# Attention scores of a decode kernel: quarters of the keys on four column groups against halves on two

## The chip, the cores and the metric

The kernel runs on one core of a Trainium2 chip. The metric is device time in microseconds (us) of that core for one launch. A core has a tensor engine (PE; its weight loads are listed apart as PEld), a vector engine (DVE), a scalar engine (ACT), GpSimd (POOL) and a sync engine (SP), which here issues all transfers; 16 DMA engines move the data. SBUF is the on-chip memory with 128 partitions; PSUM is the memory that PE writes to, in banks of 512 float32 per partition.

## The reference

One token passes four blocks, two attention layers (A) and two mixers (B), with the same weights and caches in both rounds:

```python
# A: x is (1, 1, 640); 32 heads of 192; the last W = 4096 keys of the cache
q = (x @ wq).reshape(B, Sq, Hq, Dh).transpose(0, 2, 1, 3)
scores = jnp.einsum("bhqd,bhkd->bhqk", q, k) * (Dh ** -0.5)
p = softmax(scores, axis=-1)
o = jnp.einsum("bhqk,bhkd->bhqd", p, v)
a = o.transpose(0, 2, 1, 3).reshape(B, Sq, Hq * Dh) @ wo
# B: layernorm, w1 and gelu, shifts, w2; layernorm, w3, gelu, w4
x = x + A(layernorm(x)); x = x + B(layernorm(x))
x = x + A(layernorm(x)); x = x + B(layernorm(x))
```

All tensors are bf16. With one token the shifted parts of B are zero, so the kernel computes of B only the second half (w3, gelu, w4). K and V of one head are 4096 x 192 bf16, 1536 KB each.

## The kernel before

**Storage.** Big loads go to a ring of 12 cells in SBUF, each 128 partitions x 6144 bf16 (1536 KB, one head's K or V). `take` gets a cell from the front of a queue of free cells, `give` puts it back. A load is issued by SP in the fixed order of `stream`, up to eight in flight; it waits until the last reader of its cell is done. In layer 0 the transposed K of heads 0 to 7 (`NKEEP`) is kept in eight cells, and layer 1 uses it instead of loading these heads again.

**Groups.** Heads go in eight groups of four (`QH`). Layer 0 takes the groups from the last to the first, so the kept heads are transposed in its last two groups; layer 1 from the first to the last. `attention` runs, for each group, the softmax of this group (scores done during the group before), then for each of its heads the product with V (`pv`) and, in between, the transposes and scores of the next group's heads.

**K to scores.** A cell of K has 32 keys in each partition. `transpose_quart` turns a quarter of it with one DVE instruction (L450): 128 x 768 words of 32 bit, in 32 x 32 blocks, so that a word with two neighbouring elements of a key stays whole. The result goes to a kept cell or to a quarter of the `area` cell. `scores` multiplies: the stationary operand is a 16-column block of `Qblk` (4 heads x 4 blocks of 32 keys; the other heads' columns hold zeros, so a group accumulates into one block), the moving operand are 256 elements of a turned quarter. There are `NCOL` = 6 matmuls for each quarter, and quarter q writes the 16 rows at partition 32 q of the score tile `ST_ps`. So the four quarters of a head lie in four groups of 32 partitions. T(h, half) and S(h, half) in `attention` work on two quarters at a time, and S alternates between the two. For kept heads in layer 1 one S does all four.

The tile `ST_both` (L540) is one PSUM bank, 128 partitions x 512 float32. Its left 256 columns serve one group of heads, its right 256 the next, in turn (`next_scores`).

**Softmax** (`softmax_steps`), in seven steps: `part_max`, the maximum of each row (L557, DVE); `turn_max`, a PE transpose of the 128 maxima to one row (L562); `full_max`, the maximum per head, written out again for 128 rows (L567, L572); `spread_max`, a matmul that turns it back (L580), a copy (L583), and exp with the row sums (L586, ACT); `turn_p`, a DVE transpose of P in 32 x 32 blocks, 128 x 256 bf16 (L591), and the row sums by head (L593); `swap`, 16 matmuls with 32-column parts of the identity (L605) that gather P by key into `PT`, a copy (L608), and the sums over partitions (L613); `recip`, their reciprocal.

**Values.** `pv` makes 16 matmuls of 384 columns, in four column groups (L654); DVE turns the result (L661, 128 x 384) and `o_fold` sums it (L668 or L672 and L673) into `oT`. `out_proj` and `out_row` multiply by wo.

**Order of the work.** [...] At the start of a group it is, on DVE: T(h0, 0), `part_max`, T(h0, 1), `full_max`, `turn_p`, T(h1, 0), T(h1, 1); on PE: S(h0, 0), `turn_max`, S(h0, 1), `spread_max`, a q projection and an output projection, `swap`, then `pv` of the first head, S(h1, 0), S(h1, 1), `o_fold`, `pv` of the second, S(h2, 0), and so on. Layer 1 starts with the scores of the kept heads, four of the first and four of the second group, in a row.

Of the kernel before, what the change touches and what calls it, by code (L numbers as in the profile page):

```python
# [10 lines left out]
F32 = mybir.dt.float32  # L11
U32 = mybir.dt.uint32
ACTF = mybir.ActivationFunctionType
ALU = mybir.AluOpType
AX = mybir.AxisListType
# [3 lines left out]
P = 128  # L19
# [13 lines left out]
NJ4, NGK, NM = 4, 8, 4  # L33
# [26 lines left out]
def kernel(  # L60
# [14 lines left out]
    nc = tc.nc  # L75
# [12 lines left out]
    QH = 4  # L88
    NG = H // QH
    QC = QH * Dh  # L90
    QT = QC // P
    NT = 4
    QUART = NFB * (NGK // NT) * P * 2
    FREE = NT * QUART
    scale = float(Dh) ** -0.5
    eps = 1e-5
    s0 = Sk - W
# [332 lines left out]
    area = [None, 0]  # L430
    SW = P * NGK // NT

    def transpose_quart(layer, h, q):

        if layer == 1 and h < NKEEP:
            return kept[h][:, q * QUART:(q + 1) * QUART]
        Kn = need("k", layer, h)
        NY = NFB * (NGK // NT)
        Ku = Kn[:].bitcast(U32).rearrange("p (j y b) -> p j y b", j=NJ4, b=32)
        if layer == 0 and h < NKEEP:  # L440
            if q == 0:
                kept[h] = take(("T", h))
            T = kept[h][:, q * QUART:(q + 1) * QUART]
        else:
            if area[0] is None:
                area[0] = take(("area", layer))
            T = area[0][:, area[1] * QUART:(area[1] + 1) * QUART]
            area[1] = (area[1] + 1) % NT
        Tu = T.bitcast(U32).rearrange("p (y j b) -> p j y b", y=NY, j=NJ4)
        nc.vector.transpose(Tu, Ku[:, :, q * NY:(q + 1) * NY])  # L450
        if q == NT - 1:
            give(("k", layer, h))
        return T

    def qproj_steps(c, xc, part=None, row=None):
# [29 lines left out]
        def spread():  # L485
            if row is not None:
                qT_ps = psm.tile([P, n], F32, tag="psm")
                for tl in range(n):
                    i, j = divmod(tl, n // 2)
                    nc.tensor.matmul(qT_ps[:, tl:tl + 1], lhsT=row[:, j * P:(j + 1) * P],  # L490
                                     rhs=Eq[0:33, i, 0:1], start=True, stop=True)
                held["q"] = qT_ps
            Xq = o_bytes[:, 2 * (SW + 2 * QH):][:, 0:4 * n].rearrange("p (t b) -> p t b", b=4)
            nc.vector.tensor_tensor(  # L494
                out=Xq[:], in0=held["q"][:, :].unsqueeze(2).broadcast_to([P, n, 4]),
                in1=maskq[:, :].unsqueeze(1).broadcast_to([P, n, 4]), op=ALU.mult)
            held["x"] = Xq
# [23 lines left out]

        return project, spread, repeat, block

    def scores(h, Ts, q0, ST_ps, hq):

        ng = NGK // NT
        Q = [Qblk[:, h // QH % 2, QAT[hq] + n * QSTEP:][:, 0:QW] for n in range(NCOL)]
        views = [T.rearrange("p (g f i t) -> p g f i t", f=NFB, g=ng, i=P) for T in Ts]
        for f in range(NFB):
            for t in range(2):  # L530
                n = 2 * f + t
                for i, T4 in enumerate(views):
                    r = 32 * (q0 + i)
                    nc.tensor.matmul(  # L534
                        ST_ps[r:r + QW, :].rearrange("p (g i) -> p g i", g=ng), lhsT=Q[n],
                        rhs=T4[:, :, f, :, t],
                        start=(hq == 0 and n == 0), stop=(hq == QH - 1 and n == NCOL - 1))


    ST_both = psS.tile([P, 2 * SW], F32, name="ST_ps")  # L540
    nc.vector.memset(ST_both[:], 0.0)
    turn = [0]

    def next_scores():
        turn[0] += 1
        i = turn[0] % 2
        return ST_both[:, i * SW:(i + 1) * SW]

    def softmax_steps(n, ST_ps, sc, space, bank=None):
        held = {}
        halves = space.bitcast(BF16)

        def part_max():
            pm = short("pm")
            nc.vector.tensor_reduce(out=pm[:], in_=ST_ps, op=ALU.max, axis=AX.X)  # L557
            held["pm"] = pm

        def turn_max():  # L560
            pmT_ps = psm.tile([1, P], F32, tag="psm")
            nc.tensor.transpose(pmT_ps[0:1, :], held["pm"][:, 0:1], ident[:, :])  # L562
            held["pmT"] = pmT_ps

        def full_max():
            ngm = space[0:1, SW:SW + 2 * QH]
            nc.vector.tensor_reduce(out=ngm[:], in_=held["pmT"][0:1, :].rearrange("o (q x m) -> o x q m", q=4, m=NM),  # L567
                                    op=ALU.max, axis=AX.XY, negate=True)
            held["PrT"] = halves[:, SW:2 * SW]

            wide = held["PrT"][0:1, :].bitcast(F32)
            nc.vector.tensor_scalar(  # L572
                out=wide.rearrange("o (q x m) -> o q x m", q=4, m=NM),
                in0=ngm[:].unsqueeze(1).unsqueeze(3).broadcast_to([1, 4, 2 * QH, NM]),
                scalar1=sc[0:1, 0:1], scalar2=None, op0=ALU.mult)
            held["w"] = wide

        def spread_max():
            nb_ps = psm.tile([P, 1], F32, tag="psm")
            nc.tensor.matmul(nb_ps[:], lhsT=held["w"],  # L580
                             rhs=one[0:1, :], start=True, stop=True)
            nb_sb = space[:, 289:290]
            nc.scalar.copy(nb_sb[:], nb_ps[:])  # L583
            Pr = halves[:, 0:SW]
            lpart = space[:, 288:289]
            nc.scalar.activation(out=Pr, in_=ST_ps, func=ACTF.Exp,  # L586
                                 bias=nb_sb[:, 0:1], scale=sc[:, 0:1], accum_out=lpart[:, 0:1])
            held["Pr"], held["l"] = Pr, lpart

        def turn_p():  # L590
            nc.vector.transpose(held["PrT"], held["Pr"])  # L591
            lh = space[:, 280:284]
            nc.vector.tensor_scalar(out=lh[:], in0=hm[:], scalar1=held["l"][:, 0:1], scalar2=None, op0=ALU.mult)  # L593
            held["lh"] = lh

        def swap():
            ng = NGK // NT
            if bank is None:
                PT_ps = psm.tile([P, n, NJ4, NGK], F32, tag="psm")
            else:  # L600
                PT_ps = bank[:, 0:n * NJ4 * NGK].rearrange("p (h j g) -> p h j g", j=NJ4, g=NGK)
            src = held["PrT"].rearrange("p (g j i) -> p i j g", g=ng, j=NJ4)
            for m in range(NM):
                for q in range(NT):
                    nc.tensor.matmul(PT_ps[32 * m:32 * (m + 1), :, :, ng * q:ng * (q + 1)], lhsT=Eq[:, q, :],  # L605
                                     rhs=src[:, m:QW:NM], start=True, stop=True)
            PT = big.tile([P, n, NJ4 * NGK], BF16, name="PT")
            nc.scalar.copy(PT[:].rearrange("p h c -> p (h c)"), PT_ps[:].rearrange("p h j g -> p (h j g)"))  # L608
            if bank is None:
                l_ps = psm.tile([P, QH], F32, tag="psm")  # L610
            else:
                l_ps = bank[:, 512:512 + QH]
            nc.tensor.matmul(l_ps[:], lhsT=ones, rhs=held["lh"][:], start=True, stop=True)  # L613
            held["lps"] = l_ps
            return PT

        def recip():
            lq = space[:, 284:288]
            rl = short("rl", 1, 2)
            nc.vector.scalar_tensor_tensor(out=lq[:], in0=held["lps"][:], scalar=1.0, in1=blkm[:],  # L620
                                           op0=ALU.mult, op1=ALU.mult, accum_out=rl[:, 0:1])
            nc.vector.reciprocal(rl[:], rl[:])
            return rl

        return part_max, turn_max, full_max, spread_max, turn_p, swap, recip
# [100 lines left out]
    def attention(layer, x_cur, rs_cur, x_new, z_new, rs_new, ss_new):  # L726
# [11 lines left out]
            nc.vector.tensor_scalar(out=sc[:], in0=rstd[:], scalar1=scale, scalar2=None, op0=ALU.mult)  # L738

        def T(h, half):  # L740
            for q in (2 * half, 2 * half + 1):
                if (h, q) not in Th:
                    Th[h, q] = transpose_quart(layer, h, q)

        def S(h, half, ST_ps, hq):
            if layer == 1 and h < NKEEP:
                if half == 1:
                    scores(h, [Th.pop((h, q)) for q in range(NT)], 0, ST_ps, hq)
                    give(("T", h))
                return  # L750
            scores(h, [Th.pop((h, q)) for q in (2 * half, 2 * half + 1)], 2 * half, ST_ps, hq)
            if half == 1 and layer == 0 and h == last_plain:
                give(("area", layer))
                area[0] = None
# [37 lines left out]
        for hq, h in enumerate(groups[0]):  # L792
            for half in range(2):
                if layer == 0:
                    T(h, half)
                else:
                    Th.update({(h, q): transpose_quart(layer, h, q) for q in (2 * half, 2 * half + 1)})
                S(h, half, ST, hq)
                if (hq, half) == (0, layer):
                    qb[2]()  # L800
# [317 lines left out]
```

## Time and profile before

| what | value |
|---|---|
| median of three runs | 511.95 us (511.36 to 512.05) |
| the profiled execution, its time | 511.54 us |
| its span, first to last instruction | 509.7 us |
| granted PE clock, mean | 0.723 |
| read from HBM | 214.01 MB, 420 GB/s over the span |
| score matmuls, L534 | 1536, busy 157.8 us |
| K transposes, L450 | 224, busy 201.6 us |
| PV matmuls, L654 | busy 90.2 us (largest group) |

The page divides the span into 40 slices of 12.7 us and gives for each the busy share of an engine and the rate of the transfers. A busy PE is not PE at its peak: its instructions overlap, and their ends are modelled. "Granted clock" is the share of the full PE clock. In a line of a group the fields are: source line, engine, operation, output and inputs, shape, count; then busy time and mean length in ns; then the idle time of the engine just before them and what ended it. In the lists of waits and in the chain, "DMA x" is a transfer of x that somebody waits for; in the list of transfers the last number is the median time in us from issue to landing.

### The profile page before, as it was taken

The numbers are of one execution on the slowest core, as the hardware profiler recorded it, in microseconds if no ns is written. First come the engines' busy times: TensorE is split into PE (matmuls) and PEld (weight loads), VectorE is DVE, ScalarE is ACT, GpSimd is POOL, SyncE is SP. The second block draws the span as 40 slices with busy tenths as digits, with TensorE's granted clock in tenths as the row PEclk, the third lists the DMA queues.
The fourth block names the chain that finished last, engine by engine and source line by source line (L and its number), as shares of the span: only waits on it lengthen the run. The fifth ranks groups of instructions, "written<-read, shape, count | busy, mean of one in ns | idle before, by whom it ended". The sixth has DMA issues, their size and how long they took to land.

```text
span 509.7 us, 9498 instructions
## 1 busy us (share of the span) xinstructions
PE 313.2 (61%) x4084; PEld 186.2 (37%) x4084; DVE 292.6 (57%) x604; ACT 48.9 (10%) x173; POOL 3.7 (1%) x16
## 2 busy tenths in 40 slices
PE   1056667666565555857655766767655765557685
PEld 0023333343332322534333643544322433324354
DVE  2067557666674755566723244968666656656522
ACT  1000101010010100001010101010100101001101
POOL 2000000000000000000000000000000000000000
PEclk9999756777597766576765586789887766857655
DMA  8999999999999999999999999999999999999996
GB/s 370 432 432 429 430 441 432 429 429 422 417 426 441 432 425 446 432 402 458 429 391 413 381 438 424 439 429 429 426 429 433 429 430 432 418 437 429 418 409 250
DMA packets 12014, 214.63 MB, mean 421 GB/s; under 512 B 2564, under 2 KB 3076, under 8 KB 7428
## 3 DMA queue, kind: packets, MB, share of 16 engines
q1 hardware_dynamic: 11972, 214.02, 98.5%
q8 instruction: 32, 0.52, 0.4%
q14 instruction: 10, 0.08, 0.0%
HBM read 214.01 MB, written 0.00 MB: 420 GB/s over the span
## 4 chain that ended last, share of the span: by engine, by line
DMA 60%; PE 20%; DVE 14%; issue 4%; ACT 1%; SPq 1%; DVEq 0%; ACTq 0%
DMA cell<-in_A_k_cache_dram 37%; DMA cell<-in_A_v_cache_dram 19%; DVE cell L450 9%; PE ST_ps L534 9%; PE O_ps L654 5%; DMA cell<-in_B_w_dram 4%; DVE o_sb L661 2%; PE qT_ps L480 1%; PE y_ps L1062 1%; PE nb_ps L580 1%; DVE words L557 1%; PE l_ps L613 1%; DVE V_ps L643 1%; DVE o_sb L591 1%; SPq L55 0%
## 5 line engine op out<-in xcount | busy, mean ns | idle before, releaser
L534 PE MATMUL ST_ps<-cell,Qblk 128*16 128x256 bf16 x1536 | 157.8, 364 | 110.8 <-DVE cell L450 66.6
L450 DVE STREAM_TRANSPOSE cell<-cell 128x768 uint32<-128x768 uint32 x224 | 201.6, 946 | 33.7 <-DMA cell<-in_A_k_cache_dram 31.6
L534 PEld LDWEIGHTS <-Qblk 128*16 128x16 bf16 x1536 | 84.7, 108 | 175.1 <-issue 150.2
L654 PE MATMUL O_ps<-cell,PT 128*2 128x384 bf16 x1000 | 90.2, 436 | 11.0 <-DMA cell<-in_A_v_cache_dram 9.1
L661 DVE STREAM_TRANSPOSE o_sb<-O_ps 128x384 f32<-128x384 f32 x64 | 36.7, 573 | 79.6 <-PE O_ps L654 79.5
L654 PEld LDWEIGHTS <-PT 128*2 128x2 bf16 x1024 | 41.2, 96 | 26.9 <-issue 18.7
L669 ACT ACTIVATE words<-oT_ps,words 32x6 bf16<-32x6 f32 x40 | 10.3, 257 | 163.6 <-PE oT_ps L668 150.3
L591 DVE STREAM_TRANSPOSE o_sb<-o_sb 128x256 bf16<-128x256 bf16 x15 | 6.7, 445 | 31.9 <-ACT o_sb L586 14.2
L668 PE MATMUL oT_ps<-o_sb,Lq 128*32 128x6 f32 x160 | 13.4, 192 | 10.7 <-DVE o_sb L661 10.1
L668 PEld LDWEIGHTS oT_ps<-o_sb,Lq 128*32 128x32 f32 x160 | 11.6, 137 | 20.4 <-issue 14.4
L674 ACT ACTIVATE words<-oT_ps,words 32x6 bf16<-32x6 f32 x24 | 6.2, 257 | 107.6 <-PE ST_ps L534 79.6
L480 PE MATMUL qT_ps<-words,wq_sb 128*128 128x1 bf16 x210 | 7.2, 165 | 12.9 <-DMA wq_sb<-in_A_wq_dram 12.0
L494 DVE TENSOR_TENSOR o_sb<-qT_ps,words 128x24 bf16<-128x24 f32 (+1 forms) x18 | 2.9, 163 | 20.2 <-PE qT_ps L480 17.4
L583 ACT COPY o_sb<-nb_ps 128x1 f32<-128x1 f32 x15 | 2.4, 159 | 102.2 <-PE nb_ps L580 102.2
L480 PEld LDWEIGHTS <-wq_sb 128*128 128x128 bf16 x210 | 6.8, 104 | 14.1 <-DMA wq_sb<-in_A_wq_dram 13.1
L605 PEld LDWEIGHTS <-ident 128*32 128x32 bf16 x256 | 5.8, 111 | 14.8 <-issue 14.5
L469 PE MATMUL qr_ps<-wq_sb,words 128*1 128x384 bf16 x90 | 10.7, 376 | 0.0
L700 PE MATMUL yr_ps<-cell,words 128*1 128x320 bf16 x108 | 10.4, 335 | 0.0
L673 PE MATMUL oT_ps<-o_sb,Lq 128*32 128x6 f32 x48 | 5.9, 194 | 6.8 <-DVE o_sb L672 6.8
L580 PEld LDWEIGHTS nb_ps<-words,o_sb 1*128 1x128 f32 x30 | 7.0, 287 | 7.2 <-issue 5.4
L673 PEld LDWEIGHTS oT_ps<-o_sb,Lq 128*32 128x32 f32 x48 | 5.0, 134 | 11.2 <-issue 9.1
L580 PE MATMUL nb_ps<-words,o_sb 1*128 1x1 f32 x30 | 8.2, 339 | 1.5 <-DVE o_sb L572 1.5
(159 smaller groups left out, 200.3 us busy)
## 6 DMA issues: line engine op xcount, KB each, us to landing
cell<-in_A_k_cache_dram SPq DMA_DIRECT2D x56, 1536.0 KB, 27.7
cell<-in_A_v_cache_dram SPq DMA_DIRECT2D x56, 1536.0 KB, 27.7
cell<-in_A_wo_dram SPq DMA_DIRECT2D x13, 960.0 KB, 27.5
wq_sb<-in_A_wq_dram SPq DMA_DIRECT2D x5, 1536.0 KB, 13.4
cell<-in_A_v_cache_dram SPq DMA_DIRECT2D x6, 768.0 KB, 23.7
cell<-in_B_w_dram SPq DMA_DIRECT2D x1, 1536.0 KB, 11.8
cell<-in_B_w_dram SPq DMA_DIRECT2D x2, 768.0 KB, 10.3
cell<-in_A_wo_dram SPq DMA_DIRECT2D x3, 480.0 KB, 17.0
```

Of the source, the lines that this page charges most:

```text
L450: nc.vector.transpose(Tu, Ku[:, :, q * NY:(q + 1) * NY])
L469: nc.tensor.matmul(qr_ps[32 * i:32 * i + 1, :], lhsT=xc[:, kc:kc + 1], rhs=wq_sb[:, kc, t0 * P + i * N:t0 * P + (i + 1) * N], start=(kc == ...
L480: nc.tensor.matmul(qT_ps[:, tl:tl + 1], lhsT=wq_sb[:, kc, t * P:(t + 1) * P], rhs=xc[:, kc:kc + 1], start=(kc == 0), stop=(kc == ND - 1))
L534: nc.tensor.matmul(ST_ps[r:r + QW, :].rearrange("p (g i) -> p g i", g=ng), lhsT=Q[n], rhs=T4[:, :, f, :, t], start=(hq == 0 and n == 0), s ...
L580: nc.tensor.matmul(nb_ps[:], lhsT=held["w"], rhs=one[0:1, :], start=True, stop=True)
L591: nc.vector.transpose(held["PrT"], held["Pr"])
L654: nc.tensor.matmul(O_ps[r:r + 2, :], lhsT=PT[:, hq, 2 * i:2 * i + 2], rhs=v_pair(V, h, 2 * i * Dh, 2 * Dh), start=(i < 4), stop=(i >= NB - 4))
L661: nc.vector.transpose(o_sb[:], O_ps.rearrange("p (e a c) -> p e c a", e=2, c=NA))
L668: nc.tensor.matmul(oT_ps[r, :], lhsT=Lq[:], rhs=o_sb[:, e, :, e], start=(e == 0), stop=(e == 1))
L669: nc.scalar.activation(oT[r, :], oT_ps[r, :], ACTF.Copy, scale=rl[r, 0:1])
L673: nc.tensor.matmul(oT_ps[r, :], lhsT=Lq[:], rhs=o2, start=True, stop=True)
L700: nc.tensor.matmul(yr_ps[32 * i:32 * i + 1, :], lhsT=oT[:, k:k + 1], rhs=wo_t[:, k * D + i * N:k * D + (i + 1) * N], start=(k == 0), stop= ...
```

## The change

K is turned and multiplied in halves instead of quarters, and the two groups in flight share the score bank by partitions instead of by columns:

- `NT` is 2 instead of 4. One DVE transpose turns half a head, 128 x 1536 words; a head has two of them instead of four.
- A score matmul has 512 moving columns instead of 256, and a head has 12 of them instead of 24. The half at index q0 writes 16 rows at partition ST[0] + 32 q0. So a head uses two groups of 32 partitions: 0 and 32 for one group of heads, 64 and 96 for the next.
- `ST_both` is still one bank; a group of heads has 64 partitions x 512 columns of it. `part_max`, exp and `turn_p` run on 64 partitions with 512 elements each. `turn_p` writes P turned to the other 64 partitions.
- `turn_max` turns 64 maxima, `full_max` and the spread write 64, and the sums over partitions run over 64. The short buffers of the softmax move within `o_sb`.
- `PT` comes from 8 matmuls with 64 moving columns and 64 rows, instead of 16 with 32 columns and 128 rows.

What is loaded, in which order, and the order of the steps in `attention` stay. In the core of the diff "..." marks what is left out:

```diff
-    NT = 4
-    QUART = NFB * (NGK // NT) * P * 2
-    FREE = NT * QUART
+    NT = 2
+    HP = P // 2
+    HALF = NFB * (NGK // NT) * P * 2
+    FREE = NT * HALF
...
-    def scores(h, Ts, q0, ST_ps, hq):
+    def scores(h, Ts, q0, ST, hq):
...
-                    r = 32 * (q0 + i)
+                    r = ST[0] + 32 * (q0 + i)
                     nc.tensor.matmul(
-                        ST_ps[r:r + QW, :].rearrange("p (g i) -> p g i", g=ng), lhsT=Q[n],
+                        ST_both[r:r + QW, :].rearrange("p (g i) -> p g i", g=ng), lhsT=Q[n],
                         rhs=T4[:, :, f, :, t],
...
-    ST_both = psS.tile([P, 2 * SW], F32, name="ST_ps")
+    ST_both = psS.tile([P, SW], F32, name="ST_ps")
...
-        i = turn[0] % 2
-        return ST_both[:, i * SW:(i + 1) * SW]
+        i = turn[0] % 2 * HP
+        return i, ST_both[i:i + HP, :]
...
+        at, ST_ps = ST
+        S, T = slice(at, at + HP), slice(HP - at, P - at)
...
-            nc.vector.tensor_reduce(out=pm[:], in_=ST_ps, op=ALU.max, axis=AX.X)
+            nc.vector.tensor_reduce(out=pm[S, :], in_=ST_ps, op=ALU.max, axis=AX.X)
...
-            nc.tensor.transpose(pmT_ps[0:1, :], held["pm"][:, 0:1], ident[:, :])
+            nc.tensor.transpose(pmT_ps[0:1, :], held["pm"][S, 0:1], ident[S, S])
...
+            held["PrT"] = halves[T, 0:SW]
             nc.vector.transpose(held["PrT"], held["Pr"])
...
-                    nc.tensor.matmul(PT_ps[32 * m:32 * (m + 1), :, :, ng * q:ng * (q + 1)], lhsT=Eq[:, q, :],
+                    nc.tensor.matmul(PT_ps[32 * m:32 * (m + 1), :, :, ng * q:ng * (q + 1)], lhsT=Eq[T, (HP - at) // 32 + q, :],
                                      rhs=src[:, m:QW:NM], start=True, stop=True)
...
         def T(h, half):
-            for q in (2 * half, 2 * half + 1):
-                if (h, q) not in Th:
-                    Th[h, q] = transpose_quart(layer, h, q)
+            if (h, half) not in Th:
+                Th[h, half] = transpose_half(layer, h, half)
```

## The prediction

> **What bounds the kernel now.** I read the page's first three parts, then the groups by shape, the transfers by window, the chain, and the timeline of the tensor engine (PE).
>
> ```profile
> PE 313.2 (61%) x4084; PEld 186.2 (37%) x4084; DVE 292.6 (57%) x604; ACT 48.9 (10%) x173; POOL 3.7 (1%) x16
> GB/s 370 432 432 429 430 441 432 429 429 422 417 426 441 432 425 446 432 402 458 429 391 413 381 438 424 439 429 429 426 429 433 429 430 432 418 437 429 418 409 250
> q1 hardware_dynamic: 11972, 214.02, 98.5%
> ```
>
> No compute engine is busy two thirds of the time; the transfers hold all 16 DMA engines from start to end. 214.6 MB at the usual 430 GB/s is 499 us of the 509.7 us span. So work on PE or DVE costs nothing until it releases a buffer so late that the transfer queue runs dry. What must be read is how much queue stands ahead of each release. Landing times tell it (issue to landing; windows 100 to 150 us, 249 to 250, 289 to 290 and 321 to 321.5, in this order):
>
> ```profile
> cell<-in_A_k_cache_dram SPq DMA_DIRECT2D x6, 1536.0 KB, 27.7
> cell<-in_A_v_cache_dram SPq DMA_DIRECT2D x1, 1536.0 KB, 10.9
> cell<-in_A_k_cache_dram SPq DMA_DIRECT2D x1, 1536.0 KB, 8.8
> cell<-in_A_k_cache_dram SPq DMA_DIRECT2D x1, 1536.0 KB, 13.3
> ```
>
> In steady state these transfers are issued every 3.63 us, so a landing of 27.7 means seven others in front. At 289.5 a landing takes 8.8 us, and there alone the engines visibly slack (343 GB/s in 291.9 to 295.3, below). I take 8.8 as the landing of an almost dry queue, and landing minus 8.8 as cover: 18.9 us in mid-kernel, 2.1 at 249.3, none at 289.5, 4.5 at 321.1. The cover is thin because layer 0 ends with eight cells holding kept transposed heads, so few are left to load into.
>
> Two stretches are chains of compute that wait for no data: 199.8 to 244.7 (layer 0, last groups) and 286 to 321 (start of layer 1). What the change adds there, less the cover, is lost.
>
> **The change, part by part.** Its core is the score matmuls.
>
> ```profile
> L534 PE MATMUL ST_ps<-cell,Qblk 128*16 128x256 bf16 x1536 | 157.8, 364 | 110.8 <-DVE cell L450 66.6 <-DVE words L557 38.1 <-DVE o_sb L672 4.7
> 202.01 1.45 PE L534 MATMUL ST_ps<-cell,Qblk 128*16 128x256 bf16 x12 [4.45 <-DVE words L557]
> 63.54 0.37 PE L534 MATMUL ST_ps<-cell,Qblk 128*16 128x256 bf16 x1 [1.54 <-DVE cell L450]
> 58.83 1.68 PE L534 MATMUL ST_ps<-cell,Qblk 128*16 128x256 bf16 x22
> 294.55 2.33 PE L534 MATMUL ST_ps<-cell,Qblk 128*16 128x256 bf16 x74 [0.30 <-DVE Qblk L518]
> ```
>
> (Start, length, instructions in one run.) A half of a head is 12 matmuls into two column groups (partitions r and r+32). They take 1.45 us, one alone 0.37, so (1.45-0.37)/5 = 0.216 us a pair: two groups run side by side, each a 256-column matmul per 0.216. That is at granted clock 0.50. The run of 74 has four groups at clock 1.00: (2.33-0.28)/17.5 = 0.117 us for four. So the price is columns per column group. After the change a half is 6 matmuls of 512 columns into one group: the same columns, but no partner. 6 x 0.43 = 2.6 us instead of 6 x 0.216 = 1.3 at clock 0.5: **+1.3 us a half cold, +0.65 warm**. Half as many instructions buy nothing back, since PE streams columns.
>
> Where the halves of a head are both ready, they overlap: from 58.83 on, 22 of 24 matmuls take 1.68 us, and the last two end at 60.71, 1.9 us in all, where pairs in sequence would need 12 x 0.216 + 0.2 = 2.8. I take it that the two new column groups overlap so too. [...]
>
> Prices of one step each, cold / warm:
> - (b) A later head of a group: DVE transposes both halves, PE follows. Four transposes take 3.51 us (62.55, L450); two of twice the size: 946 ns plus 768 elements at (946-727)/256 ns (768 elements at L450, 512 at L643) is 1.6 each, 3.3 in all, -0.2. Only the second half's scores are exposed: +1.3-0.2 = +1.1 / +0.45.
> - (c) The second head, whose transposes are done early: 1.9 us become 2.6+0.4 (the same stagger): +1.1 / +0.55.
> - (d) The first head: the maximum (L557) now reads 512 elements on 64 partitions instead of 256 on 128; 392 ns become some 660 by the same slope or 1 ns an element, +0.25 (0 to +0.3). In the built program the first score matmul still waits for it, though it reads the other half of the bank, so the 0.4 us of that wait are not saved. The second half stands behind the transpose of the maxima, which stands behind the first half, so both count: +2.6+0.25-0.1 = +2.7 cold; warm, 0.6 us of it fills the wait for the second transpose: +0.95. Behind it on PE queue the spread of the maximum, the next q projection and the first PV.
> - (e) The rest of the softmax: exp (L586, 564 ns for 256) at 0.8 ns an element (ACT: 468 ns for 384 at L474, 265 for 128 at L608) +0.2; the turn of P (L591, 445 ns) +0.25. PT: 8 matmuls of 64 columns for 16 of 32, equal columns, taken as 0 (-0.2, if instructions count; +0.2, if 64-row operands stall PE). +0.45.
> - (f) The eight kept heads at the start of layer 1: 24 matmuls in four groups become 12 of 512 in two: 0.7 to 1.4 us warm, 1.3 to 2.6 cold. One and a half heads run before PE warms up at 291.9: 1.5 x 1.3 + 6.5 x 0.7 = 6.5; part may fill the 0.8 us that PE idles at 296.9; I take 6.
>
> The clock decides between the ends. Windows (length, PE, PEld, DVE, ACT, POOL busy, granted clock, DMA share, GB/s):
>
> ```profile
> 66.60:70.10 3.50, 2.23 (x27) 1.21 (x23) 1.23 (x2) 0.26 (x1) 0.00 (x0) 0.50 0.99 425
> 80.30:83.70 3.40, 3.40 (x25) 1.95 (x26) 1.05 (x5) 0.81 (x3) 0.00 (x0) 0.50 1.04 448
> 83.70:87.10 3.40, 1.97 (x37) 1.09 (x33) 3.35 (x7) 0.99 (x3) 0.00 (x0) 1.00 1.07 463
> 291.90:295.30 3.40, 3.10 (x103) 2.33 (x99) 0.66 (x4) 0.12 (x1) 0.00 (x0) 0.99 0.91 343
> 199.80:244.70 44.90, 31.90 (x387) 20.29 (x387) 28.25 (x53) 3.44 (x13) 0.00 (x0) 0.62 1.00 428
> ```
>
> A stretch of 3.4 us with PE busy throughout is followed by clock 1.00; one with 65% stays at 0.50. Longer score runs fill more such stretches, so the change warms its own clock. [...]
>
> Sum, **first stretch**: it holds two of each of (b) to (e). Cold 2 x (1.1+1.1+2.7+0.45) = 10.7, warm 4.9. Now a quarter of it is warm (mean 0.62). With half warm: 7.8, less what warmth gains on today's work: a cold head step is 6.84 us (62.55 to 69.38, DVE to DVE), by 0.117 instead of 0.216 some 1.2 less; a quarter more warmth over seven such steps is -2. Less the 0.5 us that DVE waits for K at 245.7: about 5. Cover 2.1: **2.9 us lost** (ends: 0 and 8).
> **Second stretch**: (f) 6, (e) twice 0.9, (d) once 1.8, less 0.7 for warmth: 8. Cover 4.5: **3.5 lost** (0.9 with all warm and the idle filled; 5.6 cold).
> Elsewhere nothing: a cold group takes 29.4 us (52.3 to 81.7) against 31.4 of transfers (wo issues at 104.05, 135.43, 166.83) and would take 29.4+2.7+1.1+2.2+0.45 = 35.9 if it stayed cold; 4.5 over four groups is 18, just within the cover of 18.9. Without that cover it would cost those 18. In the tail the scores of the last head (477.3) release the cell for w3 later by 1.5 to 3.4, against a landing of 10.3 for half-size transfers, some 3 us of cover; taken as 0.
> Instruction fetch: 0.6 MB for 9,498 instructions; 1,792 fewer (1,536 at L534, 256 at PT) are 0.11 MB, -0.3 us.
> 2.9+3.5-0.3 = +6.1 on the profiled 511.54: **517.6 us**. The median of the runs is 0.4 above that execution, inside this.
>
> **Rivals.**
> 1. Hidden after all. PE warms up nearly everywhere; the first stretch then costs less than its cover, the second 0.9: 511.5+0.9-0.3 = 512.1. For: full windows become more frequent by (b) and (c). Against: DVE's 3.3 us per head still leave PE idle 2.3 us a head, and 257.8 to 291.9 is cold throughout. Decides at a mean clock above 0.85 in the first stretch.
> 2. PE keeps program order, so halves never overlap: (b) +0.85 more, (c) +2.2 more when cold; a half-warm group grows by some 3 us over the 31.4, and eleven groups of it less the cover give +15: 527. [...] Against: the 1.9 us.
> 3. Faster. If the scores' delay is absorbed and the shorter program frees transfers, at most the fetch (0.3) and the slack seen around 290 (about 0.8) come back: 510.4. Against: the kept heads, which gate exactly that place, get slower by (f).
>
> **How the numbers follow.** My forecast 0.65, rival 1 0.22, rival 2 0.08, rival 3 0.05. Runs spread 0.7 us, so 0.2%, 1.0 us, is what can be told from no change. Slower 0.65+0.08, within 0.2% 0.22, faster 0.05. The range goes from between rivals 3 and 1 (511.2) to the cold ends of both stretches (511.5+8+5.6 = 525); the forecast's own range is 513 to 525.
>
> **What would show it.** Right: L534 768 times, each about twice as long, PE busy up; GB/s dips between 244 and 268 and between 289 and 325, with landings near 8 us; the clock higher between 60 and 240. Steps: the kept heads' scores take 1.3 to 1.4 us each when warm; part maximum about 0.66, exp 0.76, turn of P 0.7 us. Wrong: steady 430 GB/s through both stretches (rival 1); scores of the second half starting only after the first half's last matmul (rival 2); landings below 25 us already at 150 (the cover in mid-kernel not enough).

## The result and the profile after

| | before | after |
|---|---|---|
| median | 511.61 us (6 runs, 511.36 to 512.05) | 535.25 us (6 runs, 533.06 to 536.82) |
| ratio | | 1.0457, 95% interval 1.0428 to 1.0487 |
| profiled execution | 511.54 us | 536.82 us, span 535.0 |
| granted PE clock, mean | 0.723 | 0.783 |

The kernel became slower by 23.6 us, four times the 6.1 of the prediction and outside its range. The page of the kernel after (busy times, transfer rate in 40 slices of 13.4 us, the transfer queue, the costliest groups):

```profile
PE 358.1 (67%) x3188; PEld 154.4 (29%) x3188; DVE 296.3 (55%) x492; ACT 51.7 (10%) x173; POOL 3.7 (1%) x16
GB/s 364 459 412 442 432 426 415 431 459 424 415 429 455 416 386 340 345 222 349 299 371 369 410 376 389 441 403 430 428 427 439 432 425 425 442 434 420 431 396 229
q1 hardware_dynamic: 11972, 214.02, 95.6%
L535 PE MATMUL ST_ps<-cell,Qblk 128*16 128x512 bf16 x768 | 224.5, 501 | 83.6 <-DVE cell L451 49.3
```

The transfers no longer hold their engines to the end. The rate falls below 400 in ten of the slices from 187 to 334 us, to 222 at the worst. This is longer and earlier than the two dips that were predicted. How the queue got there is seen in the landing times (issue to landing, windows 100 to 150 and 249 to 250 us):

```profile
cell<-in_A_v_cache_dram SPq DMA_DIRECT2D x6, 1536.0 KB, 17.5
cell<-in_A_k_cache_dram SPq DMA_DIRECT2D x5, 1536.0 KB, 18.1
cell<-in_A_v_cache_dram SPq DMA_DIRECT2D x1, 1536.0 KB, 9.0
```

A landing took 27.7 us there before. So already in mid-kernel a third of the queue is gone, though the rate still is 430: the loss is being prepared where nobody sees it. A V cell issued between 196 and 206 us lands in 8.8, the prediction's own mark of an almost dry queue. Windows of the end of layer 0, first of before, then of after (length, PE, PEld, DVE, ACT, POOL busy, granted clock, DMA share, GB/s):

```profile
200.00:245.00 45.00, 31.90 (x387) 20.29 (x387) 28.37 (x53) 3.44 (x13) 0.00 (x0) 0.62 0.99 425
```

```profile
200.00:245.00 45.00, 31.68 (x269) 14.20 (x263) 24.37 (x36) 2.57 (x9) 0.00 (x0) 0.77 0.80 299
```

The DMA engines are idle a fifth of this stretch. PE has the same busy time and a higher clock than before, and is late all the same.

**When it becomes late.** The copy in `spread_max` (L583, now L585) is a good clock of the groups, since it runs once in each. Its starts in layer 0, in us, read from the two traces:

| group | 1 | 2 | 3 | 4 | 5 | 6 | 7 | 8 |
|---|---|---|---|---|---|---|---|---|
| before | 52.8 | 82.3 | 111.2 | 141.3 | 172.7 | 205.7 | 237.2 | 260.0 |
| after | 57.6 | 91.3 | 125.4 | 159.5 | 193.7 | 226.2 | 260.3 | 280.9 |
| later by | 4.8 | 9.0 | 14.2 | 18.2 | 21.0 | 20.5 | 23.1 | 20.9 |

In layer 0 the whole delay is made before 194 us. In layer 1 it grows once more, to 37.9 us at its fourth group, and falls back to 24.7 at the last copy (506.6 us, before 481.9). From group 2 to group 5 the copies of after are 34.1, 34.1 and 34.2 us apart, more than the 31.4 us that a group's transfers take.

**Why a group takes 34.1 us.** In the trace of after the granted clock changes 79 times, always between 0.50 and 1.00, and each change comes a whole multiple of 3.413 us after the one before. Windows of after, cut at such multiples:

```profile
111.64:115.06 3.42, 3.42 (x22) 1.11 (x22) 1.57 (x2) 0.00 (x0) 0.00 (x0) 0.50 1.07 460
115.06:118.47 3.41, 1.37 (x15) 0.47 (x10) 2.16 (x3) 0.51 (x2) 0.00 (x0) 1.00 1.07 461
118.47:121.88 3.41, 2.37 (x6) 0.61 (x5) 2.75 (x3) 0.00 (x0) 0.00 (x0) 0.50 0.94 404
121.88:125.30 3.42, 3.42 (x11) 0.98 (x10) 0.46 (x2) 0.00 (x0) 0.00 (x0) 0.50 0.87 374
...
135.54:138.95 3.41, 1.06 (x10) 0.40 (x5) 2.65 (x3) 0.26 (x1) 0.00 (x0) 1.00 1.04 447
138.95:142.37 3.42, 3.42 (x16) 1.02 (x14) 1.31 (x2) 0.00 (x0) 0.00 (x0) 0.50 1.00 431
142.37:145.78 3.41, 1.09 (x20) 0.46 (x18) 2.26 (x3) 0.26 (x1) 0.00 (x0) 1.00 0.80 346
145.78:149.19 3.41, 3.38 (x20) 1.11 (x20) 1.69 (x2) 0.00 (x0) 0.00 (x0) 0.50 0.94 404
...
152.60:156.01 3.41, 2.42 (x6) 0.63 (x5) 2.62 (x3) 0.00 (x0) 0.00 (x0) 0.50 1.07 454
```

Read the PE busy time (the first number behind the length) against the clock. In these rows full windows (busy 3.38 to 3.42) are cold (clock 0.50) and nearly empty ones (1.06 to 1.37) are warm (1.00). A burst of scores fills a cold window; a warm one follows; that one falls on PE's wait for the next K to be turned, and the next one is cold, just when the next scores come. From 29.7 us to the end of this trace, 31 of 33 cold windows with PE busy for more than 3.3 us are followed by a warm one, and all 22 warm ones with less than 1.4 by a cold one. The row at 152.60 is the one at 118.47 again: ten windows, 34.13 us, one group. Of the 144 score matmuls that the trace has between 80 and 182 us, 88% start in a cold window (before: 70% of 324), though the mean clock of that stretch is 0.75 in both. Two score runs of that group and what follows (start, length, instructions):

```profile
119.51 2.72 PE L535 MATMUL ST_ps<-cell,Qblk 128*16 128x512 bf16 x6 [2.10 <-DVE words L561]
122.15 0.26 PE L566 MATMUL pmT_ps<-ident,words 64*1 64x64 f32 x1
122.34 2.73 PE L535 MATMUL ST_ps<-cell,Qblk 128*16 128x512 bf16 x6
...
131.38 0.82 PE L657 MATMUL O_ps<-cell,PT 128*2 128x384 bf16 x16
```

Both halves of the first head run fully cold, 2.7 us each, one behind the other, as the prediction's price (d) has it.

### The profile page after: what moved, and what is told of

It is laid out like the page before. It is cut to its first block, busy times and chain, and to the rows that moved or that the text cites. A ratio compares the mean times of both kernels' runs of the same rounds, so it can differ in the third digit from the quotient of the medians.

```text
span 535.0 us, 7568 instructions
## 1 busy us (share of the span) xinstructions
PE 358.1 (67%) x3188; PEld 154.4 (29%) x3188; DVE 296.3 (55%) x492; ACT 51.7 (10%) x173; POOL 3.7 (1%) x16
## 4 chain that ended last, share of the span: by engine, by line
PE 44%; DMA 24%; DVE 22%; issue 6%; ACT 3%; SPq 1%; ACTq 0%
PE ST_ps L535 28%; DVE cell L451 11%; DMA cell<-in_A_v_cache_dram 11%; DMA cell<-in_A_k_cache_dram 9%; PE O_ps L657 9%; DMA cell<-in_B_w_dram 4%; DVE o_sb L664 4%; ACT o_sb L588 2%; DVE o_sb L594 2%; DVE words L561 2%; PE y_ps L1064 1%; PE l_ps L616 1%; PE PT_ps L608 1%; DVE wx_sb L713 1%; PE nb_ps L582 1%
## 5 line engine op out<-in xcount | busy, mean ns | idle before, releaser
L535 PE MATMUL ST_ps<-cell,Qblk 128*16 128x512 bf16 x768 | 224.5, 501 | 83.6 <-DVE cell L451 49.3
L451 DVE STREAM_TRANSPOSE cell<-cell 128x1536 uint32<-128x1536 uint32 x112 | 194.6, 1754 | 8.7 <-DMA cell<-in_A_k_cache_dram 4.4
L535 PEld LDWEIGHTS <-Qblk 128*16 128x16 bf16 x768 | 67.0, 104 | 207.5 <-issue 172.8
L657 PE MATMUL O_ps<-cell,PT 128*2 128x384 bf16 x1000 | 100.6, 399 | 10.0 <-DMA cell<-in_A_v_cache_dram 8.1
L594 DVE STREAM_TRANSPOSE o_sb<-o_sb 64x512 bf16<-64x512 bf16 x15 | 10.6, 706 | 44.3 <-ACT o_sb L588 44.3
L671 PE MATMUL oT_ps<-o_sb,Lq 128*32 128x6 f32 x160 | 12.6, 187 | 10.4 <-DVE o_sb L664 9.8
L671 PEld LDWEIGHTS oT_ps<-o_sb,Lq 128*32 128x32 f32 x160 | 10.2, 127 | 18.7 <-issue 13.6
L585 ACT COPY o_sb<-nb_ps 64x1 f32<-64x1 f32 x15 | 2.3, 154 | 115.9 <-PE nb_ps L582 115.9
L561 DVE TENSOR_REDUCE words<-ST_ps 64x1 f32<-64x512 f32 x16 | 10.8, 674 | 3.9 <-PE ST_ps L535 3.8
L588 ACT ACTIVATE o_sb<-ST_ps,o_sb,words 64x512 bf16<-64x512 f32 x15 | 11.6, 773 | 0.5
L481 PEld LDWEIGHTS <-wq_sb 128*128 128x128 bf16 x210 | 6.6, 100 | 14.4 <-DMA wq_sb<-in_A_wq_dram 13.1
L519 DVE TENSOR_TENSOR Qblk<-Qrep_ps,words 128x48 bf16<-128x48 f32 (+1 forms) x36 | 5.4, 192 | 8.1 <-PE Qrep_ps L502 7.9
## 6 DMA issues: line engine op xcount, KB each, us to landing
cell<-in_A_k_cache_dram SPq DMA_DIRECT2D x56, 1536.0 KB, 18.2
cell<-in_A_wo_dram SPq DMA_DIRECT2D x13, 960.0 KB, 15.8
wq_sb<-in_A_wq_dram SPq DMA_DIRECT2D x5, 1536.0 KB, 13.4
cell<-in_A_v_cache_dram SPq DMA_DIRECT2D x6, 768.0 KB, 23.6
cell<-in_B_w_dram SPq DMA_DIRECT2D x1, 1536.0 KB, 13.4
```

Of the source, the lines that this page charges most:

```text
L481: nc.tensor.matmul(qT_ps[:, tl:tl + 1], lhsT=wq_sb[:, kc, t * P:(t + 1) * P], rhs=xc[:, kc:kc + 1], start=(kc == 0), stop=(kc == ND - 1))
L535: nc.tensor.matmul(ST_both[r:r + QW, :].rearrange("p (g i) -> p g i", g=ng), lhsT=Q[n], rhs=T4[:, :, f, :, t], start=(hq == 0 and n == 0), ...
L561: nc.vector.tensor_reduce(out=pm[S, :], in_=ST_ps, op=ALU.max, axis=AX.X)
L588: nc.scalar.activation(out=Pr, in_=ST_ps, func=ACTF.Exp, bias=nb_sb[:, 0:1], scale=sc[S, 0:1], accum_out=lpart[:, 0:1])
L657: nc.tensor.matmul(O_ps[r:r + 2, :], lhsT=PT[:, hq, 2 * i:2 * i + 2], rhs=v_pair(V, h, 2 * i * Dh, 2 * Dh), start=(i < 4), stop=(i >= NB - 4))
L671: nc.tensor.matmul(oT_ps[r, :], lhsT=Lq[:], rhs=o_sb[:, e, :, e], start=(e == 0), stop=(e == 1))
```

## The experiments

The theory (A) was that the scores' lost partner column group makes a group of heads longer than its transfers; the rivals are named in the expectations. Sixteen kernels were run. "Given back" is the difference of a median from 535.25. The runs of after spread from 533.06 to 536.82, and the intervals of k_layer1_only and k_first_only touch that of after (1.043 to 1.049), so the small amounts are the least sure.

| run | what differs | median, us | ratio (95%) |
|---|---|---|---|
| k_halves_only | before, K turned in halves | 511.43 | 1.000 (0.999 to 1.001) |
| k_softmax_twice | before, three softmax steps twice | 515.50 | 1.007 (1.006 to 1.009) |
| k_scores_twice | before, scores twice | 522.19 | 1.021 (1.017 to 1.025) |
| k_halves_scores_twice | both of halves and scores | 521.86 | 1.019 (1.016 to 1.022) |
| k_both_twice | scores and softmax twice | 552.77 | 1.081 (1.071 to 1.091) |
| k_all_twice | halves, scores, softmax | 549.10 | 1.073 (1.064 to 1.081) |
| k_half_terms | after, half the contraction everywhere | 511.22 | 0.999 (0.998 to 1.000) |
| k_first_only | the same for heads 28 to 31 of layer 0 | 531.66 | 1.040 (1.034 to 1.045) |
| k_middle_only | for heads 12 to 27 of layer 0 | 523.40 | 1.024 (1.021 to 1.027) |
| k_end_only | for heads 0 to 11 of layer 0 | 530.88 | 1.036 (1.031 to 1.041) |
| k_layer1_only | for layer 1 | 533.43 | 1.041 (1.038 to 1.043) |
| k_split | after, 512 columns as 2 x 256 | 537.73 | 1.050 (1.047 to 1.052) |
| k_turn_ahead | after, K turned ahead in layer 0 | 514.40 | 1.006 (1.004 to 1.008) |
| k_filled | after, extra matmuls in PE's waits | 516.65 | 1.010 (1.002 to 1.018) |
| k_before_ahead | before, K turned ahead | 511.93 | 1.000 (0.999 to 1.001) |
| k_halves_ahead | before, halves and turned ahead | 512.24 | 1.000 (0.999 to 1.002) |

**Which part of the change costs.** First the parts one by one.

k_halves_only:

```diff
-        NY = NFB * (NGK // NT)
+        NY = 2 * NFB * (NGK // NT)
...
-        nc.vector.transpose(Tu, Ku[:, :, q * NY:(q + 1) * NY])
+        nc.vector.transpose(Tu, Ku[:, :, half * NY:(half + 1) * NY])
...
+        return [T[:, 0:QUART], T[:, QUART:2 * QUART]]
```

> The kernel before, with only K's turning changed: DVE turns each half in one instruction, as the kernel after does; the scores stay on four column groups of 256 columns. Theory A (what costs is that a half's scores have lost their partner column group, so that a group of heads takes 34 us of compute against 31.4 of transfers): time as before, 511 to 512.5, groups spaced 31.4 us. Rival C (the coarser turning is what costs, since PE has to wait longer for its first piece): 520 or more, DVE-bound gaps on PE.

511.43 us. DVE's transposes are those of after (112 of 1757 ns), and the time is that of before. The coarser turning alone costs nothing.

k_half_terms:

```diff
                 n = 2 * f + t
+                if n not in terms:
+                    continue
...
-                        start=(hq == 0 and n == 0), stop=(hq == QH - 1 and n == NCOL - 1))
+                        start=(hq == 0 and n == 0), stop=(hq == QH - 1 and n == terms[-1]))
...
+            terms = range(0, NCOL, 2) if True else range(NCOL)
```

> The kernel after, with the scores summing only the first of the two values in each word, 3 matmuls a half instead of 6: half of the contraction of the scores is left out, everything else (512 columns, 64 partitions, one column group a half, the wider softmax) stays. Theory A: a half is back at 1.3 us cold, groups are spaced 31.4 us again, 512 to 515. Rival B (the softmax on 64 partitions is what costs): 530 or more, since its steps are all still there.

511.22 us, all of the loss given back, with the softmax on 64 partitions and the one-group layout still there. Its score matmuls, and its landings between 100 and 150 us:

```profile
L537 PE MATMUL ST_ps<-cell,Qblk 128*16 128x512 bf16 x384 | 140.6, 543 | 117.5 <-DVE cell L451 70.5
```

```profile
cell<-in_A_k_cache_dram SPq DMA_DIRECT2D x6, 1536.0 KB, 27.7
```

Half the matmuls of after, each as wide as there, and the queue is whole again at 27.7. So the wider softmax alone costs nothing, as long as the transfers set the pace, and the time of the scores is needed for the loss.

k_scores_twice and k_softmax_twice:

```diff
-                for i, T4 in enumerate(views):
+                for k, i, T4 in [(k, i, T4) for k in range(times) for i, T4 in enumerate(views)]:
...
-            nc.vector.tensor_scalar(out=sc[:], in0=rstd[:], scalar1=scale, scalar2=None, op0=ALU.mult)
+            nc.vector.tensor_scalar(out=sc[:], in0=rstd[:], scalar1=scale / 2, scalar2=None, op0=ALU.mult)
```

```diff
-            nc.vector.tensor_reduce(out=pm[:], in_=ST_ps, op=ALU.max, axis=AX.X)
+            for _ in range(2):
+                nc.vector.tensor_reduce(out=pm[:], in_=ST_ps, op=ALU.max, axis=AX.X)
```

(and so for the exponential and `turn_p`)

> The kernel before, with every score matmul issued twice and the scale halved: four column groups of 256 columns stay, and so does the softmax on 128 partitions, but each column group gets as many columns as a half has in the kernel after. Theory A: 2.6 us a half cold, groups spaced 33 to 34 us, the queue dry after 190 us, 525 to 537. Rival B (softmax): 511 to 513. If instructions rather than columns had a price, more than 537, since there are four times as many as after.

> The kernel before, with three softmax steps issued twice: the partition maxima, the exponential and the turning of P. That adds about 0.39 + 0.56 + 0.45 = 1.4 us to each group's chain, against some 0.7 that the wider softmax of the kernel after adds. Theory A: 511.5 to 514. Rival B: 530 or more.

522.19 and 515.50. Neither theory has these numbers: the scores are the larger part, but 10.7 us is under theory A's 525, and the softmax gives 4.0 where A had at most 2.5. In k_scores_twice a column group gets as many columns as in after, and yet the groups of heads stay under 31.4 us (below); 27% of its score matmuls between 80 and 182 us start in a cold window, where after has 88%. So the columns alone, as theory A first had it, don't make the loss; this kernel lacks the wider softmax, and its scores are mostly warm. Three further kernels put the parts together:

> The kernel before, with every score matmul issued twice (scale halved) and part maximum, exponential and turning of P issued twice. Scores alone cost 10.7 us, softmax alone 4.0. Theory H (a softmax step is cheap while transfers set the pace and paid in full once compute does): 1.4 us over the groups that are bound by compute, 530 to 538. Rival F (what separates 522 from 535 is the clock of the scores): the sum or little more, 523 to 528.

> The kernel before, with every score matmul issued twice (scale halved) and K turned in halves by one instruction each. Turning alone cost nothing while transfers set the pace. If it costs nothing on a chain bound by compute either: 520 to 524, as with quarters. If the coarser turning is what separates 522 from 535: 530 or more.

> The kernel before, with K turned in halves, every score matmul issued twice (scale halved) and the three softmax steps issued twice: each part of the change by a stand-in that keeps four column groups and 128 partitions. If the parts (columns per group, turning, softmax) are the whole of the change: 533 to 540. If the clock's phase at the scores is a part of its own: 523 to 530, with a granted clock above 0.85 between 80 and 190 us.

552.77, 521.86 and 549.10. The turning costs nothing in any company. Scores and softmax cost 41 us together where they cost 10.7 and 4.0 alone. Theory H holds in kind (the softmax step, cheap while transfers set the pace, is dear once compute does), and even its range was too low; rival F, that the sum would be kept, falls. k_all_twice is above both ranges of its expectation and 14 us above after, so these stand-ins don't add up to the change. Windows of k_both_twice, one group length each:

```profile
80.00:114.00 34.00, 22.77 (x318) 14.72 (x314) 20.41 (x40) 3.59 (x12) 0.00 (x0) 0.80 1.00 427
114.00:148.00 34.00, 22.78 (x318) 14.64 (x313) 20.36 (x40) 3.60 (x12) 0.00 (x0) 0.80 1.01 434
148.00:182.00 34.00, 22.78 (x317) 14.67 (x312) 20.38 (x40) 3.59 (x12) 0.00 (x0) 0.80 1.00 426
```

Three groups alike to a hundredth of a us: its softmax copies are 34.1 us apart each time, again ten times 3.413. In k_scores_twice they are 28.3, 33.2, 28.3 and 30.4 us apart from group 2 to group 6, mean 30.0, with a clock of 0.84 to 0.96 between 80 and 182 us, under the 31.4 of the transfers. So 1.4 us of softmax make a step of 4 in the period. In after the step is smaller (part maximum, exp and turn add 0.28, 0.21 and 0.26 us), and it lands on the same period.

k_split:

```diff
-                    nc.tensor.matmul(
-                        ST_both[r:r + QW, :].rearrange("p (g i) -> p g i", g=ng), lhsT=Q[n],
-                        rhs=T4[:, :, f, :, t],
...
+                    for a in (0, ng // 2):
+                        b = a + ng // 2
+                        nc.tensor.matmul(
+                            ST_both[r:r + QW, a * P:b * P].rearrange("p (g i) -> p g i", g=ng // 2), lhsT=Q[n],
+                            rhs=T4[:, a:b, f, :, t],
...
```

> The kernel after, with each score matmul of 512 columns split into two of 256 columns in the same column group: 24 matmuls a head as before, the same columns, still no partner within a half. Theory A (columns per column group are the price): 532 to 537. Rival G (the length of one matmul is the price, since long ones block PE for others): 511 to 520.

537.73, 0.7 above theory A's range. As many instructions as before, and no gain: what counts is the columns of a column group, not the size of a matmul (its 1536 score matmuls keep PE busy for 228.1 us, the 768 of after for 224.5).

**Where it is paid.** The edit of k_half_terms, for some heads only:

```diff
+            terms = range(0, NCOL, 2) if layer == 0 and 12 <= h < 28 else range(NCOL)
```

(`h < 12`, `h >= 28`, and `layer == 1` in the others)

> The kernel after, with half of the contraction of the scores left out (3 matmuls a half) for heads 12 to 27 of layer 0 alone; these scores run between about 60 and 190 us. The heads scored after 190 us and all of layer 1 are as in the kernel after. Theory A1 (the delay that fills up before 190 us is what is paid later): nearly all of the 21 us of lag that the kernel after has at 194 us goes, and what is left is the later stretches' own: 515 to 522, the softmax copy of the fifth group at about 175 instead of 193.7. Rival D (the prediction's own reckoning, the delay in mid-kernel is within its cover and the loss is made at the end of layer 0 and the start of layer 1): 530 to 536.

> The kernel after, with half of the contraction of the scores left out for heads 0 to 11 of layer 0 alone, whose scores run from about 180 to 275 us; heads 12 to 31 and layer 1 are as after. Theory A1: the lag of 21 us is there at 194 us as before and can't be made up, since the kernel before has no slack there either beyond a few us: 527 to 533. Rival D: 514 to 520.

> The kernel after, with half of the contraction of the scores left out in layer 1 alone; layer 0 is as after. The two kernels that left out the middle and the end of layer 0 gave back 11.9 and 4.4 us of the 23.6; if the parts add up, 7.3 remain for layer 1 and the first group together: 527 to 531. Theory A1 has the lag of some 21 us at 281 us unchanged and the further growth to 38 us between 300 and 402 us gone. If layer 1 makes up what it loses by itself (after's lag falls from 38 back to 25 by the end), the time stays at 533 to 536.

> The kernel after, with half of the contraction of the scores left out for heads 28 to 31 of layer 0 alone, the first four heads scored, before any softmax. Middle, end and layer 1 gave back 11.9, 4.4 and 2.0 of 23.6 us. If the parts add up, the first group holds the remaining 5.3: 529 to 531.5, and the first softmax copy comes at about 53 instead of 57.6 us, with that lead kept to the end. If the start is hidden by transfers: 534 to 536.

Given back: 11.9 (middle), 4.4 (end), 1.8 (layer 1), 3.6 (first group), together 21.6 of 23.6. The middle alone is half of it, though the rate showed no loss there; it ended 1.4 us above A1's range, and its copy at group 5 is at 177.2, 4.5 after before's; half of that is there from the first group (55.1, 2.2 late). A landing of k_middle_only between 100 and 150 us takes 27.7, and its transfer rate (40 slices of 13.0 us) has a shorter dip:

```profile
GB/s 363 434 442 436 415 455 423 436 423 433 429 424 436 424 432 430 425 423 276 356 399 360 402 392 430 433 419 434 434 423 432 431 428 430 422 437 427 416 411 202
```

k_end_only shows the reverse: its lag at group 5 is 20.2 us, and with the old score times from there on it is still 18.0 at the last copy (15.5 at the best). What is late at 194 us is hardly made up later. Layer 1 makes up most of its own delay, the last case of its expectation: k_layer1_only is never more than 22.2 us behind before there, where after gets to 37.9, and yet its last copy is only 4.5 us ahead of after's. k_first_only is 0.2 above the range for a first group whose delay is kept; its first copy is at 52.7, and its last is 6.0 ahead of after's.

**The clock, and the wait.** Two kernels leave the scores of after as they are.

```diff
-                elif layer == 1 and nxt and 0 < hq < 3:
+                elif nxt and 0 < hq < 3 and not (layer == 0 and hurry):
                     T(nxt[0][1], 0)
```

> The kernel after, with the first half of K of the next head turned ahead of P times V in layer 0 too (until now in layer 1 alone), for two of the four heads of a group: PE no longer waits 1.75 us for that turning, twice a group. The score matmuls stay as after. Theory A1: the group falls from 34.0 to about 31 us, the transfers set the pace again, 513 to 520. Rival E (PE itself is full with the scores): no gain, 533 to 536.

```diff
+        def fill(count):
+            for _ in range(count if layer == 0 else 0):
+                nc.tensor.matmul(V_bank[0:32, 1930:2042], lhsT=ident[:, 0:32], rhs=ident[:, 0:112],
+                                 start=True, stop=True)
...
+                    fill(5)
                     S(h0, 0, ST_n, 0)
...
+                        fill((6, 1)[half] if hq else 0)
                         S(h2, half, ST_n, q2)
```

> The kernel after, with 19 matmuls a group of layer 0 (128x112 float32, results not used) put in front of the scores where PE waits for K's turning and for the partition maxima; nothing else changed, so PE has more work. Theory F (the scores run at clock 0.50 because PE's waits cool it: each score run falls into a cold window, and the warm window goes to the next wait): the granted clock rises from 0.75 to above 0.9 between 80 and 190 us, a half's scores fall from 2.7 to about 1.5 us, the group to 31.4 us or less, 515 to 525. Rival E (PE has too much work): the fillers add up to 19 x 0.2 to 0.37 us a group, 535 to 560.

514.40 and 516.65. Turning K ahead cuts a wait of PE of 2.3 us in two heads of a group to 1.3 or 1.4 and gives back 20.9 us; it raises the clock too (0.84 to 0.87 between 114 and 182 us), so this run alone doesn't part the wait from the clock. The second does: 19 extra matmuls a group of 267 ns, 5 us of PE work, and the kernel is 18.6 us faster. Its windows, then its score matmuls between 80 and 182 us, then those of after:

```profile
114.00:148.00 34.00, 25.62 (x223) 12.86 (x223) 20.89 (x32) 4.01 (x12) 0.00 (x0) 0.90 1.01 436
148.00:182.00 34.00, 22.95 (x220) 11.47 (x217) 22.68 (x34) 4.34 (x14) 0.00 (x0) 0.90 1.00 428
```

```profile
L535 PE MATMUL ST_ps<-cell,Qblk 128*16 128x512 bf16 x156 | 41.2, 443 | 15.7 <-DVE cell L451 10.7 <-DVE words L561 4.3
```

```profile
L535 PE MATMUL ST_ps<-cell,Qblk 128*16 128x512 bf16 x147 | 52.1, 596 | 20.1 <-DVE cell L451 14.0 <-DVE words L561 6.0
```

The clock is 0.90 where after has 0.75, a score matmul's mean length falls from 596 to 443 ns, 23% of 156 start cold instead of 88%, and groups follow each other by 30.8 us (the softmax copies of group 1 to 5, 55.0 to 178.1). With the same columns, a group takes 34.1 us where 88% of the scores start cold, and 30.8, under the 31.4 of the transfers, where 23% do. That the period sits on whole windows is a reading of the traces. From group 1 to group 6 the copies of k_softmax_twice and k_halves_scores_twice are 30.6 to 30.9 us apart (nine windows are 30.7); those of k_both_twice, which has the softmax of the one and the scores of the other, are 34.0 to 34.1 apart from group 2 on (ten windows). But in k_split they are 31.4 to 35.6 apart, and it is no faster than after, so the loss doesn't need the fixed period.

k_before_ahead and k_halves_ahead carry the first diff of this part over to before:

> The kernel before (quarters, four column groups), with the first half of K of the next head turned ahead of P times V in layer 0 too. Its transfers are busy 98.5% and the 16 engines idle only 0.8 us between 280 and 300 us before the end, so at most about 1 us is to be had: 510.4 to 511.8.

> The kernel before, with K turned by half heads in one instruction each (scores still on four column groups) and the first half of the next head turned ahead of P times V in layer 0 too: the one part of the change that cost nothing, with the repair that took the kernel after from 535 to 514. By the same bound as the run beside it: 510.4 to 511.8.

511.93 and 512.24, a little above their range, as the kernel before was beside them (512.03): no change. The transfers leave nothing to gain, so no version here beats the kernel before.

## Why the prediction was wrong, step by step

**The failed step** is "Elsewhere nothing", with its reason: "4.5 over four groups is 18, just within the cover of 18.9". It counts cover at 100 to 150 us for the middle, and the cover of 2.1 at 249.3 again for the first stretch. But both are one queue. In before, the queue of 27.7 us is what layer 0's end lives on while eight cells are being kept; the 2.1 are what is left of it when it starts full: landings of before take 24 to 26 us at 190 to 200, 14 to 17 at 210 to 230, 10.9 at 249. Delay in mid-kernel spends it ahead of time, and the end then runs dry by that much more. A cover that is needed later isn't cover. The middle, set at 0, gave back 11.9 us. The prediction's own sentence "Without that cover it would cost those 18" leads to 517.6 + 18 = 535.6; that this is so near 535.25 is partly chance, as the other terms show.

**The group that opens the kernel** wasn't priced at all. It made 4.8 us of lag, and was worth 3.6.

**First stretch, 2.9 lost.** The end of layer 0 gave back 4.4. Its delay was well sized: in k_middle_only the lag grows from 4.5 (group 5) to 9.8 (group 7), 5.3 against "about 5". Too large was the cover subtracted from it: of 5.3 us, 4.4 were lost.

**Second stretch, 3.5 lost.** Layer 1 gave back 1.8. The kept heads were slowed as priced (below), but the transfers made most of it good later on.

**The prices** held for the most part. Columns per column group: k_split and k_half_terms bear it out. (f): 48 matmuls of four kept heads in 5.57 us, 1.4 each when warm; all eight take 310.51 to 326.27, 15.8 us, against 10.5 before, +5.2 for 6. (d) and (e): from the first head's turning to the first product with V 14.4 us (116.97 to 131.38) against 11.5 (76.40 to 87.89), +2.9 for 3.15 cold. (e): part maximum 674 ns for some 660, exp 773 for 764, turn of P 706 for 695, PT's 8 matmuls 0.44 us for 0.46. (b) was too dear: heads in the loop are 7.2 us apart (109.76 to 116.97) against 6.84, +0.35, nearer its warm value, though the half's turning took 1.75 us where 1.6 was reckoned. (c) was too cheap: the second head's scores take 3.5 us (132.03 to 135.53) for 3.0.

**The clock.** "Longer score runs fill more such stretches, so the change warms its own clock" is true at the end of layer 0 (0.77 for 0.62), not in mid-kernel (0.75, where before had 0.70 to 0.80), and false of the scores there, which run cold. "Half warm" was the wrong kind of average: the clock of the score runs was wanted.

**The rivals.** Rival 1 (hidden): falls. Rival 2 (PE keeps program order, halves never overlap) has a time of 527 that is nearer than the forecast, but no run shows that order. In the second head of a group the scores of one half are issued behind those of the other:

```profile
132.03 2.67 PE L535 MATMUL ST_ps<-cell,Qblk 128*16 128x512 bf16 x10
134.47 0.63 PE L535 MATMUL ST_ps<-cell,Qblk 128*16 128x512 bf16 x1
134.90 0.63 PE L535 MATMUL ST_ps<-cell,Qblk 128*16 128x512 bf16 x1
```

The twelve start within 2.87 us, nearly all of it at clock 0.50, where eleven steps of 0.43 in sequence would take 4.7. So the second half starts before the first is done, against rival 2. In the kept heads the code issues the two halves in turns, and two column groups take as long as one:

```profile
310.51 2.73 PE L535 MATMUL ST_ps<-cell,Qblk 128*16 128x512 bf16 x12 [0.28 <-DVE Qblk L519]
```

(The single half is the 2.72 us at 119.51 above; the clock is 0.50 in both.) Rival 3 (faster): falls. Of what the prediction said would prove it wrong, one came true word for word, "landings below 25 us already at 150": 18.1.

## What to carry to other kernels

Cover read at one place of a trace is money to be spent once: before setting a delay in the middle against it, ask which later stretch lives on the same queue, and follow the balance to the end. Where compute and transfers are as near each other as here (30.0 us a group in k_scores_twice against 31.4), a step that is cheap alone may cost its full length, and more, once another edit has made compute the bound (the doubled softmax steps: 4.0 us alone, 30.6 on top of the doubled scores); so cost edits together. And take the clock where the costly instructions run, not the mean: in after the mean was 0.75 between 80 and 182 us, but 88% of the scores started at 0.50, and cutting PE's wait for K (2.3 us to 1.3 or 1.4) or filling it gave back 20.9 and 18.6 us, the second with 5 us more PE work a group.

## What the runs showed of the hardware

- **Busy work made the kernel faster.** 5 us more PE work a group and 18.6 us less time (k_filled). In the warm windows shown above, where PE was busy 1.06 to 1.37 of 3.41 us, the next window was cold each time, though PE's longest wait between 100 and 156 us was 2.35. The period of a group was 34.0 to 34.2 us in after and, with other edits, in k_both_twice; in k_end_only and k_layer1_only, whose code is that of after in these groups, the three stretches of 34 us from 80 us on are alike (PE busy 23.17 to 23.52 us, clock 0.75 in each).
- **Matmuls that stand later in the program started earlier.** In after, the second half's scores stand ahead of the next product with V in the program, and yet the two start in turns, nine of the product's sixteen matmuls before the last of these scores at 108.12 us (timeline of PE):

```profile
107.27 0.63 PE L535 MATMUL ST_ps<-cell,Qblk 128*16 128x512 bf16 x1
107.28 0.50 PE L657 MATMUL O_ps<-cell,PT 128*2 128x384 bf16 x3
107.70 0.63 PE L535 MATMUL ST_ps<-cell,Qblk 128*16 128x512 bf16 x1
107.70 0.49 PE L657 MATMUL O_ps<-cell,PT 128*2 128x384 bf16 x3
```

- **Transfers were slower while the queue was almost dry, besides idling.** In the windows of 200 to 245 us above, before moved 425 GB/s at a DMA share of 0.99, and after 299 at 0.80, which is 429 against 374 for a full share. The packets of 48 KB that started between 190 and 240 us took 38.0 ns per KB in before and 42.2 in after. What makes them longer was not tried.
